# Attention and routed experts on one core: keys and queries turned by 64x64 products instead of transposes

## The chip, the cores and the metric

The kernel runs on one core of a Trainium2 chip. The core has engines that work side by side: TensorE (PE in the profile; PEld are its weight loads), VectorE (DVE), ScalarE (ACT), GpSimd (POOL) and SyncE (SP), which here only issues transfers. Products leave TensorE through PSUM, a memory of eight banks of 512 floats on each of 128 partitions; the operands lie in SBUF. The metric is the device time of one execution in microseconds (us). Three runs of the kernel before gave 433.92, 434.18 and 436.34 us; the median, 434.18, is its time here. One more execution was profiled.

## The reference

Two stages. The first is attention for 8 batches and 8 heads, 576 tokens, head width 64, causal by blocks of 64 tokens:

```python
scores = scale * np.matmul(q, k.transpose(0, 1, 3, 2))
mask = block_i >= block_j                      # blocks of 64 tokens
attn = softmax(where(mask, scores, -1e9))
out  = attn @ v
```

The second takes the 512 values of each token (its 8 heads side by side) and routes the token to one of 8 experts. `logits = x @ w_gate` choose a fresh expert; a local gate, a sigmoid of `x @ w_local`, decides per token whether it takes the fresh one or that of the token before it, so choices run on along the sequence. The chosen expert is two products with a ReLU between them:

```python
h = np.maximum(x[b, s] @ w1[e], 0.0)
out[b, s] = p[e] * (h @ w2[e])                 # p: softmax of the logits
```

All inputs and the output are float32.

## The kernel before

**Pairs and slots.** Two heads of one batch make a pair; there are 32 pairs and the main loop has one slot for each (`for i in range(NPAIR)`), four slots to a batch. The two heads lie on partitions 0 to 63 and 64 to 127 of a tile, so the products of both run in different parts of the 128x128 array. A slot i does, in TensorE's order: the values product of pair i-1 (`values`, L937), scores of pair i in three units (`scores`, L901 and L903; L901 is a small product that puts a large negative number where the mask is), the scores of the last 64 tokens (`last_scores`, L923), the transposes of keys and queries of pair i+1 (`transposes`, L860 and L856), and then a task of the batch before. ACT takes the exponentials of the scores out of PSUM (L913, L926), and copies the finished values (L941) and the turned keys and queries (L851). DVE adds the exponentials of the chunks into one tile (L949), for the row sums.

**Keys and queries.** Scores need both with the head's 64 numbers on the partitions, but they arrive with tokens on the partitions. `load_qk` issues the loads on SP: 512 tokens as [128 partitions, 2 heads, 4 tokens, 64], partition p holding tokens 4p to 4p+3, and the last 64 tokens ("the tail") of keys and queries in a small tile `qkl`. The large ones land in `staged`, a part of the second expert weights' tile `w2_bf` that isn't loaded yet. Two copies on POOL (`arrange`, L822) put the four tokens outermost, so that both heads of one token index make a 128x128 block. TensorE turns eight such blocks (L856) into a PSUM pair `kq` and the tail (L860) into the tile `po`. DVE copies the tail out (L862), ACT the rest (L851); that copy (`back_in_order`) reads in a row and writes every fourth float, because token 4s+j stands in block j. `qkTs[i % 2]` holds the result.

**PSUM.** The eight banks are three pairs under the name `sc` that go round, and `po` with two banks: the tail in its first columns, the last scores, the values. A wait is made between engines that touch the same bank of one tile. In a slot without more work the pairs go to the three score units and `kq`; a task takes the next ones. `bank_of` hands out banks: it takes a new pair when none is half used, or always for a step of the routing (names that begin with `rt`), and gives its two halves in turn. `half.clear()` forgets a half that is left.

**Tasks and routing steps.** `tasks(i)` gives by the quarter r of the batch: r = 0 and 2 a gate product (`half_batch`, L703), r = 1 the logits (L725) and rows of tiles 0 and 1, r = 3 the rows of tiles 2 and 3 and then of tile 4 (`rows_out`, L717), each with its transposes. Batch 0 has none but that of r = 2. The routing itself (`early`, `tokens`, `slots_first`) is a generator whose DVE pieces are put into the slots by weight; a piece that begins with work of TensorE waits for a call of `steps.tensor()`, of which a slot has two, one ahead of the task and one behind it. Such steps are L330, L340, L350, L363, L497.

**Weights.** `load_weights` brings one layer of one expert, 1 MB as bfloat16, over POOL's queue, in every second slot from slot 2 on. On that queue it stands behind `arrange`.

**Before and behind the loop.** Ahead of the loop, pair 0 is loaded, arranged by DVE and ACT (L1045), turned, and copied in four parts (L1061). Slot 1 has another order (`swap`): its scores come ahead of the values of pair 0. After the loop the tiles of 128 routed tokens pass through the experts (L1011, L1169); this part is the same in both kernels.

Of the kernel before, what the change touches and what calls it, by code (L numbers as in the profile page):

```python
# [62 lines left out]
def kernel(  # L63
# [11 lines left out]
    nc = tc.nc  # L75
# [29 lines left out]
    def load_weights(e, layer):  # L105
        if layer == 0:
            nc.gpsimd.dma_start(
                out=w1_bf[:, e * WE:(e + 1) * WE].rearrange("p (do f) -> p do f", f=F),
                in_=moe_w1[e].rearrange("(do di) f -> di do f", di=P))
        else:  # L110
            nc.gpsimd.dma_start(
                out=w2_bf[:, e * WE:(e + 1) * WE].rearrange("p (fo d) -> p fo d", d=Dm),
                in_=moe_w2[e].rearrange("(fo fi) d -> fi fo d", fi=P))

# [658 lines left out]
    with tc.tile_pool(name="atn_const", bufs=1) as cst, \  # L773
# [15 lines left out]
        def staged_of(i):  # L789
            return second if i == 1 else staged  # L790
# [8 lines left out]
        def load_qk(i):  # L799
# [16 lines left out]

        def arrange(i, copies):
            if i >= NPAIR:
                return
# [30 lines left out]
        def back_in_order(i, parts, ps, copy):  # L850
            copy(qkTs[i % 2][:, parts, :512].rearrange("p a (s j) -> p a j s", j=4),  # L851
                 ps.rearrange("p a (j s) -> p a j s", j=4))

        def turn_part(i, part, ps, js=range(4)):
            for j in js:
                nc.tensor.transpose(ps[:, j * P:j * P + P],  # L856
                                    raws[i][1 + part][:, j].rearrange("s h d -> s (h d)"), id_f)

        def turn_tail(i):
            nc.tensor.transpose(po[:, TAIL:TAIL + P],  # L860
                                raws[i][0].rearrange("s h d -> s (h d)"), id_f)
            nc.vector.tensor_copy(qkTs[i % 2][:, :, 512:S],  # L862
                                  po[:, TAIL:TAIL + P].rearrange("p (a s) -> p a s", a=2))

        def transposes(i, copy, ahead=0):
# [5 lines left out]
            for j in range(9):  # L871
                if j == ahead:
                    turn_tail(i)
                if j < 8:
                    turn_part(i, j // 4, ps[:, j // 4], (j % 4,))
            back_in_order(i, slice(0, 2), ps, copy)
# [474 lines left out]
```

## Time and profile before

| what | value |
|---|---|
| median of three runs | 434.18 us |
| time of the profiled execution | 430.82 us |
| its span, first to last instruction | 429.0 us |
| TensorE clock granted, mean | 0.999 |
| busy: PE, PEld | 412.7, 292.6 us |
| busy: DVE, ACT, POOL | 255.6, 264.2, 162.5 us |
| the 30 ACT copies of turned keys and queries (L851) | 63.1 us |
| the 61 POOL copies that arrange them (L822) | 40.0 us |
| the 256 transposes of keys and queries (L856) | 34.0 us busy |

How to read it: a row of the groups has line, engine, operation, out<-in by the program's names, the shape, the number of instructions, then the time the group was busy, the mean of one in ns, and the idle time of its engine ahead of it with what ended that. `128*128` or `64*64` is the part of the array that a product uses. PE's times of one matmul hold its latency, so neighbours overlap, and a float32 product shows as two matmuls. The chain of waits follows back from the last instruction to what released it; the timeline merges neighbours of a kind and gives start, duration and, in brackets, idle time. `w_bf` stands for both weight tiles, `staged` among them.

### The profile page before, as it was taken

What the parts mean: (1) busy time and instruction counts of PE and PEld (TensorE: products, weight loads), DVE (VectorE), ACT (ScalarE), POOL (GpSimd) and SP (SyncE); (2) the same over time, 40 slices, a digit from 0 to 9 for tenths busy, and PEclk for the clock granted to TensorE, in tenths of its full rate; (3) what the DMA queues carried; (4) which work ended last, traced back from release to release, by engine and by line L of the source; (5) the groups of instructions that cost most, each with busy time, mean ns of one, the idle gap of its engine ahead of it and who ended that gap; (6) DMA issues with size and microseconds to landing.
All of it is one profiled execution on the core that took longest, in us unless ns stands there. A gap on an engine that the chain in (4) does not pass through costs nothing.

```text
span 429.0 us, 13472 instructions
## 1 busy us (share of the span) xinstructions
PE 412.7 (96%) x5285; PEld 292.6 (68%) x5306; DVE 255.6 (60%) x558; ACT 264.2 (62%) x409; POOL 162.5 (38%) x181
## 2 busy tenths in 40 slices
PE   8999999999999999999999999899989999999995
PEld 7666767667667666676665767667767777777763
DVE  3363654565366386867899977698798433333320
ACT  4779668757776776566675667634445555555553
POOL 1216111221311121103113143016685788888843
PEclk9999999999999999999999999999999999999999
DMA  6578979989979999698998899957474555575541
GB/s 187 125 169 183 174 171 212 177 196 174 191 169 202 186 193 181 130 149 187 205 162 202 173 181 226 148 117 139 125 160 130 135 159 138 148 147 153 126 113 74
DMA packets 114366, 69.90 MB, mean 163 GB/s; under 512 B 77567, under 2 KB 106751, under 8 KB 114304
## 3 DMA queue, kind: packets, MB, share of 16 engines
q1 hardware_dynamic: 96896, 38.07, 39.3%
q0 software_dynamic: 17408, 30.96, 36.9%
q8 instruction: 44, 0.72, 0.7%
q14 instruction: 18, 0.15, 0.1%
HBM read 66.88 MB, written 14.70 MB: 190 GB/s over the span
## 4 chain that ended last, share of the span: by engine, by line
PE 76%; DVE 9%; DMA 6%; ACT 4%; issue 3%; POOL 1%; POOLq 0%; SPq 0%; DVEq 0%; ACTq 0%
PE o L937 19%; PE sc L903 16%; PE ps_h L1011 12%; PE ps_y L1169 11%; PE trg L703 5%; DMA out_dram<-y,idx 5%; PE kq L856 4%; PE trx L717 4%; ACT Pc L913 3%; DVE S L949 3%; PE o L860 2%; DMA xT<-xg 1%; PE sc L901 1%; PE trl L725 1%; PE idle L1032 1%
## 5 line engine op out<-in xcount | busy, mean ns | idle before, releaser
L822 POOL COPY w_bf<-w_bf 128x512 f32<-128x512 f32 x61 | 40.0, 668 | 197.1 <-PE kq L856 86.4
L949 DVE TENSOR_TENSOR S<-S,Pc 128x896 f32<-128x896 f32 (+3 forms) x128 | 90.2, 705 | 14.3 <-PE o L937 8.9
L903 PE MATMUL sc<-qkT 64*64 64x224 f32 (+6 forms) x1536 | 90.6, 366 | 0.0
L1220 DVE COPY w1c<-w_bf 128x4096 bf16 x36 | 44.9, 1246 | 55.9 <-PE ps_h L1011 52.8
L1011 PEld LDWEIGHTS <-w1c 128*128 128x128 bf16 x1152 | 67.2, 98 | 10.2 <-DVE w1c L1220 1.5
L1169 PE MATMUL ps_y<-w_bf,hT 128*128 x283 | 67.6, 379 | 1.1
L1011 PE MATMUL ps_h<-xT,w1c 128*128 128x128 bf16 x1088 | 66.3, 219 | 2.1 <-DMA xT<-xg 1.1
L1177 POOL DMA_INDIRECT out_dram<-y,idx x38 | 58.7, 1545 | 22.6 <-issue 9.8
L903 PEld LDWEIGHTS sc<-qkT 64*64 64x64 f32 x1536 | 59.8, 133 | 7.8
L913 ACT ACTIVATE Pc<-sc 128x448 f32<-128x448 f32 (+1 forms) x96 | 63.8, 703 | 0.0
L851 ACT COPY qkT<-kq 128x1024 f32<-128x1024 f32 x30 | 63.1, 2103 | 0.7 <-PE kq L856 0.7
L941 ACT COPY oT<-o 128x576 f32<-128x576 f32 x32 | 20.5, 639 | 69.2 <-PE o L937 66.4
L1014 ACT ACTIVATE hT<-ps_h 128x512 bf16<-128x512 f32 x76 | 45.3, 597 | 23.9 <-PE ps_h L1011 23.2
L653 POOL DMA_INDIRECT xg<-x_rows,idx x38 | 45.5, 1198 | 37.2 <-DVE ltmp_g L378 16.1
L937 PE MATMUL o<-Pc,v 128*64 128x320 f32 (+2 forms) x512 | 57.3, 366 | 0.0
L1174 ACT ACTIVATE y<-ps_y,xg 128x512 f32<-128x512 f32 x38 | 26.2, 689 | 43.7 <-PE ps_y L1169 38.5
L913 ACT ACTIVATE S<-sc 128x576 f32<-128x576 f32 x64 | 41.7, 652 | 15.3 <-PE o L923 11.8
L937 PEld LDWEIGHTS o<-Pc,v 128*64 128x64 f32 x512 | 34.6, 137 | 24.1
L1169 PEld LDWEIGHTS <-hT 128*128 128x128 bf16 x304 | 28.2, 98 | 27.7 <-issue 0.5
L937 PE MATMUL o<-S,v 128*64 128x256 f32 (+1 forms) x256 | 38.1, 418 | 0.9 <-DVE qkT L862 0.9
L856 PE MATMUL kq<-id_f,w_bf 128*128 128x128 f32 x256 | 34.0, 276 | 0.0
L862 DVE COPY qkT<-o 128x128 f32<-128x128 f32 x32 | 9.3, 290 | 37.9 <-PE o L860 37.7
(288 smaller groups left out, 416.0 us busy)
## 6 DMA issues: line engine op xcount, KB each, us to landing
w_bf<-in_moe_w_dram POOLq DMA_DIRECT2D x16, 1024.0 KB, 10.5
w_bf<-in_k_dram SPq DMA_DIRECT2D x32, 256.0 KB, 3.5
w_bf<-in_q_dram SPq DMA_DIRECT2D x32, 256.0 KB, 5.0
v<-in_v_dram SPq DMA_DIRECT2D x64, 128.0 KB, 4.2
x_rows<-xg SPq DMA_DIRECT2D x24, 128.0 KB, 3.6
qkl<-in_k_dram SPq DMA_DIRECT2D x32, 32.0 KB, 5.4
qkl<-in_q_dram SPq DMA_DIRECT2D x32, 32.0 KB, 4.1
vl<-in_v_dram SPq DMA_DIRECT2D x32, 32.0 KB, 3.6
```

The costliest lines, as they stand in the source:

```text
L653: st = nc.gpsimd.indirect_dma_start(out=x, out_offset=None, in_=x_dram[:rows], in_offset=bass.IndirectOffsetOnAxis(ap=row_of(ph, j), axis= ...
L851: copy(qkTs[i % 2][:, parts, :512].rearrange("p a (s j) -> p a j s", j=4), ps.rearrange("p a (j s) -> p a j s", j=4))
L856: nc.tensor.transpose(ps[:, j * P:j * P + P], raws[i][1 + part][:, j].rearrange("s h d -> s (h d)"), id_f)
L903: nc.tensor.matmul(to[:, col + skip:col + n], lhsT=t[r, 0, k0:k0 + ST], rhs=t[r, 1, q0 + skip:q0 + n], start=True, stop=True)
L913: nc.scalar.activation(exps_at(i, c, q0, n, rows), ps[rows, :, col:col + n], func=AF.Exp, scale=scale_attn)
L937: nc.tensor.matmul(po[64 * h:64 * h + 64, VO + q0:VO + q0 + n], lhsT=vv, rhs=exps_at(i, c, q0, n, slice(0, P))[:, h, :], start=(c == 0), s ...
L949: nc.vector.tensor_add(Ss[i][rows, :, P * c:], Ss[i][rows, :, P * c:], Pc[i % 2][rows, :, POS[c]:POS[c] + n])
L1011: nc.tensor.matmul(ps[:, fo, :], lhsT=w[:, ko * F + f0:ko * F + f0 + P], rhs=xT[:, ko, :], start=(ko == 0), stop=(ko == KO1 - 1))
L1014: relu[0] = nc.scalar.activation(hT[:, half * (FO // 2):(half + 1) * (FO // 2), :], ps, func=AF.Relu)
L1169: nc.tensor.matmul(ps, lhsT=hT[:, fo, :], rhs=w2_bf[:, bass.ds(ev + fo * Dm, Dm)], start=(fo == 0), stop=(fo == FO - 1))
L1177: st = nc.gpsimd.indirect_dma_start(out=out_flat, out_offset=bass.IndirectOffsetOnAxis(ap=row_of(ph, j), axis=0), in_=y, in_offset=None, b ...
L1220: ended["w"] = nc.vector.tensor_copy(w, w1_bf[:, bass.ds(ev[i], WE)])
```

## The change

1. `arrange` is gone, ahead of the loop too, and with it POOL's copies and the second staging place; `staged` now has four places for raw keys and queries, those of even and of odd pairs.
2. The transposes of 128x128 blocks become products with a 64x64 identity (`flip`). `turn_part` makes four for each part and token index: two halves of the partitions (r) by two heads (h). Each reads the raw block as it was loaded, uses one 64x64 quarter of the array, and writes 64 columns, every fourth float, of bank r. So the tokens come out in order.
3. The tail is turned by four such products into the first and the last columns of `po`, one in each of its banks, and copied by ACT in place of DVE.
4. The large copy reads and writes runs of 256 floats.
5. `bank_of` no longer takes a new pair for a routing step; the halves are forgotten only ahead of the two calls of `steps.tensor()`. So a step and the task behind it share a pair. In quarter 3 tile 4 comes first.
6. `load_weights` gets a wait for the slot's large copy (`kept[0]`).

```diff
-    def load_weights(e, layer):
+    def load_weights(e, layer, behind=None):
...
+        if behind is not None:
+            tc.add_manual_dep(st.ins, behind.ins.name, mybir.DependencyInfo(
+                mybir.DependencyClass.Sync, mybir.DependencyReason.DATA),
+                reason="spread over the slots")
...
-        staged, second = (w2_bf[:, e * WE:(e + 1) * WE].bitcast(F32).rearrange(
-            "p (u c) -> p u c", u=4) for e in (E - 1, E - 2))
+        staged = w2_bf[:, (E - 1) * WE:E * WE].bitcast(F32).rearrange("p (u c) -> p u c", u=4)
...
-                m = staged_of(i)[:, j].rearrange("p (h j d) -> p h j d", h=2, j=4)
+                m = staged[:, 2 * (i % 2) + j].rearrange("p (h j d) -> p h j d", h=2, j=4)
...
-        def arrange(i, copies):
-            for j in range(2):
-                m = staged_of(i)[:, 2 + j].rearrange("p (j h d) -> p j h d", j=4, h=2)
-                copies[j](m, raws[i][1 + j].rearrange("p h j d -> p j h d"))
-                raws[i][1 + j] = m
...
-            if not half or nm.startswith("rt"):
-                half.clear()
+            if not half:
...
-        def back_in_order(i, parts, ps, copy):
-            copy(qkTs[i % 2][:, parts, :512].rearrange("p a (s j) -> p a j s", j=4),
-                 ps.rearrange("p a (j s) -> p a j s", j=4))
+        def flip(out, src, rows):
+            nc.tensor.matmul(out, lhsT=src, rhs=id_f[rows, rows], start=True, stop=True)
+
+        quarters = [(r, h, slice(64 * r, 64 * r + 64), slice(64 * h, 64 * h + 64))
+                    for r in range(2) for h in range(2)]
 
         def turn_part(i, part, ps, js=range(4)):
             for j in js:
-                nc.tensor.transpose(ps[:, j * P:j * P + P],
-                                    raws[i][1 + part][:, j].rearrange("s h d -> s (h d)"), id_f)
+                for r, h, rows, to in quarters:
+                    flip(ps[to, r].rearrange("p (a s j) -> p a j s", a=2, j=4)[:, part, j],
+                         raws[i][1 + part][rows, h, j], rows)
 
         def turn_tail(i):
-            nc.tensor.transpose(po[:, TAIL:TAIL + P],
-                                raws[i][0].rearrange("s h d -> s (h d)"), id_f)
-            nc.vector.tensor_copy(qkTs[i % 2][:, :, 512:S],
-                                  po[:, TAIL:TAIL + P].rearrange("p (a s) -> p a s", a=2))
+            tail = po.rearrange("p (a s) -> p a s", s=P)[:, 0::7, :ST]
+            for r, h, rows, to in quarters:
+                flip(tail[to, r], raws[i][0][rows, h], rows)
+            nc.scalar.copy(qkTs[i % 2][:, :, 512:S], tail)
...
-            back_in_order(i, slice(0, 2), ps, copy)
+            kept[0] = copy(qkTs[i % 2][:, :, :512].rearrange("p a (r s) -> p r a s", r=2),
+                           ps.rearrange("p r (a s) -> p r a s", a=2))
...
             if r == 3 and b:
-                return [[lambda t=t: rows_out(b - 1, t) for t in (2, 3)],
-                        [lambda: rows_out(b - 1, 4)]]
+                return [[lambda: rows_out(b - 1, 4)],
+                        [lambda t=t: rows_out(b - 1, t) for t in (2, 3)]]
...
-            turn_part(0, part, ps[:, 0])
-            for s0, s1 in ((0, FIRST[part]), (FIRST[part], P)):
-                copies[part](
-                    qkTs[0][:, part, 4 * s0:4 * s1].rearrange("p (s j) -> p j s", j=4),
-                    ps[:, 0].rearrange("p (j s) -> p j s", j=4)[:, :, s0:s1])
+            turn_part(0, part, ps)
+            for r in range(2):
+                copies[part](qkTs[0][:, part, QA * r:QA * r + QA],
+                             ps[:, r, QA * part:QA * part + QA])
         turn_tail(0)
         idle_products(2)
-        arrange(1, (nc.vector.tensor_copy, nc.gpsimd.tensor_copy))
...
+            half.clear()
             steps.tensor()
             steps.vector(2.0)
             for group in tasks(i):
-                half.clear()
...
+            half.clear()
             steps.tensor()
...
-            arrange(i + 2, [nc.gpsimd.tensor_copy] * 2)
...
-                load_weights(*divmod(wload, 2))
+                load_weights(*divmod(wload, 2), behind=kept[0])
```

More of the change, by code (lines that the diff above doesn't have):

```diff
@@ L1039 @@
         copies = (nc.vector.tensor_copy, nc.scalar.copy)
-        for part in range(2):
-            raw, m = raws[0][1 + part], staged[:, 2 + part].rearrange(
-                "p (j h d) -> p j h d", j=4, h=2)
-            for n, j in enumerate((slice(0, 2), slice(2, 4))):
-                copies[part * (1 - n)](m[:, j], raw[:, :, j].rearrange("p h j d -> p j h d"))
-            raws[0][1 + part] = m
         load_qk(1)
```

12 lines of the change are left out of this document (4 added, 8 removed).

## The prediction

> **What bounds the kernel now.** I read the page first (busy times and the chain that ended last), then the chain of waits in order of time for two slots of the attention stage, then the timeline of one slot, the groups by shape and the list of waits. TensorE (PE) is busy nearly always and carries the chain:
>
> ```profile
> span 429.0 us, 13472 instructions
> PE 412.7 (96%) x5285; PEld 292.6 (68%) x5306; DVE 255.6 (60%) x558; ACT 264.2 (62%) x409; POOL 162.5 (38%) x181
> PE 76%; DVE 9%; DMA 6%; ACT 4%; issue 3%; POOL 1%; POOLq 0%; SPq 0%; DVEq 0%; ACTq 0%
> ```
>
> The change lies in the attention stage, where PE walks through 32 slots of about 8.5 us. The chain in one slot (start, duration, what):
>
> ```profile
> 115.72 0.26 PE o L860
> 115.98 0.87 PE kq L856 x8
> 116.85 0.67 PE trl L725 x6
> 117.52 0.04 issue
> 117.56 1.09 PE trx L717 x8
> 118.65 2.85 PE o L937 x28
> ```
>
> Behind the scores come the tail transpose (L860) and the eight key and query transposes (L856), then the task of the slot and the values product (L937); only 0.04 us is not PE. So what decides is how long PE takes from its last score to its last key or query transpose, 0.26 + 0.87 = 1.13 us, and who waits next. The timeline of the slot before it (start, duration, engine, line):
>
> ```profile
> 105.15 0.33 PE L923 MATMUL o<-qkT 64*64 64x64 f32 x4
> 105.27 1.08 PE L903 MATMUL sc<-qkT 64*64 64x288 f32 x16
> ...
> 106.60 0.33 ACT L926 ACTIVATE Pc<-o 64x64 f32<-64x64 f32 x2
> 107.15 0.33 PE L860 MATMUL o<-id_f,qkl 128*128 128x128 f32 x1
> 107.32 1.04 PE L856 MATMUL kq<-id_f,w_bf 128*128 128x128 f32 x8
> 107.50 1.45 ACT L913 ACTIVATE Pc<-sc 128x448 f32<-128x448 f32 x2
> 108.28 0.16 PEld L703 LDWEIGHTS trg<-oT,wg 128*32 128x32 f32 x8 [0.17 <-issue]
> 108.83 2.16 ACT L851 COPY qkT<-kq 128x1024 f32<-128x1024 f32 x1
> 110.03 1.19 PE L937 MATMUL o<-S,v 128*64 128x256 f32 x8
> ```
>
> **Products in place of transposes.** A transpose is one instruction. A float32 product shows as two passes: L923 has two products in a slot and four matmul rows. So 8 + 1 transposes become 32 + 4 products, 72 passes with 72 weight loads: 18 passes on each of the four 64x64 tiles. From the first L923 row to the next line is 0.12 us, in which each of two tiles makes two passes of 64 columns: 0.06 us a pass, loads included. The streaming alone comes from the slope of two shapes, and whether four tiles run side by side from a third answer, for 9.20 to 9.30 us:
>
> ```profile
> L903 PE MATMUL sc<-qkT 64*64 64x288 f32 x384 | 44.8, 415 | 0.0
> L903 PE MATMUL sc<-qkT 64*64 64x128 f32 x128 | 13.3, 284 | 0.0
> ...
> 9.27 0.47 PE L903 MATMUL sc<-qkT 64*64 64x288 f32 x4
> L903 PE MATMUL sc<-qkT 64*64 64x288 f32 x4 | 0.5, 453 | 0.0
> ```
>
> (415 - 284) / 160 = 0.82 ns a column, 52 ns for 64. Four products of 453 ns fit into 0.47 us, so all four tiles start within 0.02 us. I take 56 ns, between 52 and 60: 18 x 0.056 = 1.01 us in place of 1.13, a gain of 0.12 (0.05 to 0.19). Part of it is that the new products have the tile shape of the scores before them.
>
> Does the sequencer bring 144 instructions in 1.01 us, 7 ns each? The eight L703 loads take 0.16 us, of which one lasts 0.11: 0.05 us for seven steps, 7 ns. The other end is the 0.12 us behind L923's first row, four passes and four loads, 15 ns each; but there the streaming of two tiles sets the pace. I take the first and keep the other for the rivals.
>
> The new products write every fourth float of a PSUM bank; no row shows such a write. Below, it is free; above, the nearest row is the copy that writes SBUF at the same step:
>
> ```profile
> L851 ACT COPY qkT<-kq 128x1024 f32<-128x1024 f32 x30 | 63.1, 2103 | 0.7 <-PE kq L856 0.7
> L913 ACT ACTIVATE Pc<-sc 128x1024 f32<-128x1024 f32 x32 | 33.0, 1031 | 0.0
> L913 ACT ACTIVATE Pc<-sc 128x448 f32<-128x448 f32 x64 | 34.5, 538 | 0.0
> L862 DVE COPY qkT<-o 128x128 f32<-128x128 f32 x32 | 9.3, 290 | 37.9 <-PE o L860 37.7
> ```
>
> 2103 against 1031 ns for as many elements, a factor of 2.04: a pass of 0.11 us, 16 x 0.056 = 0.90 us more a slot. I take the free end: bf16 products stream two columns, 8 bytes a partition, in the time in which a float32 pass streams one. The row for it:
>
> ```profile
> 289.05 1.07 PE L1011 MATMUL ps_h<-S,w1c 128*128 128x128 bf16 x16
> ```
>
> About 1.07/16 = 0.067 us for 128 columns with the last one's latency in it, 0.52 ns a column against 0.82. So a bank takes 8 bytes a partition in 1.04 ns there, and a stepped pass would ask it for one float in 0.82 ns: nearly the same number of places in the same time. The Trainium skill (PSUM — Partial Sum Buffer, Specifications (TRN2)) says that PSUM has cachelines of 8 bytes and that "any non-contiguous AP slows matmuls significantly". By that rule the sum would be that of the first rival below; by the bf16 row a stepped pass touches one line where bf16 touches one too, and stays at 0.056. No run here shows a stepped product.
>
> How much of 0.12 us reaches the end depends on the slot. In slots with a gate task (quarter 0 and 2 of a batch, 15 of them) only PE is on the chain: 15 x 0.12 = 1.8 us. In quarter 1 the row task waits for the exponentials (the 0.04 us above), so nothing is gained; quarter 3 fills two banks and then needs the same buffer: nothing.
>
> **The copies.** ACT's 2.10 us copy becomes contiguous, 1.03 us. The tail copy leaves DVE (0.29) for ACT: by the two L913 rows 0.86 ns an element over 155 ns, 0.27 us for 128. ACT's queue: exponentials to 108.95, tail 109.22, keys and queries 110.25 rather than 110.99. The next scores come when the values product is through, 110.03 + 2.85 = 112.9, so this hides, as does POOL's copying (61 x 0.67 us), which no PE row waits for. What is new: the values product writes the banks that the tail copy reads and now waits for ACT, behind the exponentials. With a task that is covered (109.22 against 110.03). Slot 3 has none:
>
> ```profile
> 33.11 1.04 PE L856 MATMUL kq<-id_f,w_bf 128*128 128x128 f32 x8
> 33.34 1.46 ACT L913 ACTIVATE Pc<-sc 128x448 f32<-128x448 f32 x2
> 34.07 1.19 PE L937 MATMUL o<-S,v 128*64 128x256 f32 x8
> ```
>
> Exponentials end at 34.80, the copy at 35.07, and 0.04 us later the product: 1.0 us lost, once (0 if the dependence isn't made). The tail, now in two banks, must wait for both L926, which end at 106.93; PE comes to it at 107.15 today, 0.12 earlier at most then. Nothing.
>
> **Routing steps.** PE's idle time in the stage (total, times, longest):
>
> ```profile
> PE trx L717 <- ACT Pc L913: 2.3, 4, 0.8
> PE trg L703 <- ACT Pc L913: 2.0, 4, 0.6
> PE o L937 <- DVE qkT L862: 0.9, 2, 0.8
> PE rtr L363 <- ACT qkT L851: 0.8, 2, 0.4
> ```
>
> Three bank pairs go round. Today a routing step takes the second score pair and the task behind it the third, whose exponentials end last. Sharing the pair, the gate task starts at once: 2.0 us. For the row tasks only the short tile 4, put first, fits beside the step: four transposes at 0.87/8 = 0.11, 0.43 us of each wait, 1.7 in all. The wait for L862 was DVE being late with the tail copy, 0.8 gone. L363 waits for the key and query copy, which ends 0.74 earlier: 0.5 of 0.8. Sum 5.0 us (from 2, if the next wait takes over, to 6). With the pair shared, both halves must be read before the fourth next user; DVE reads within 2 us and the next use is a slot away: nothing.
>
> **The start.** Pair 1 is turned in slot 0, copied by DVE, and slot 1 begins:
>
> ```profile
> 8.63 0.34 ACT Pc L926 x2
> 9.01 0.34 PE o L860
> 9.67 1.97 DVE qkT L851
> 11.69 0.22 PE sc L901 x2
> ```
>
> The DVE copy ends at 11.64 and lets slot 1 start. It loses the tail copy ahead of it (0.29) and, at L913's ratio, half of its 1.97: up to 1.3 us, and PE could start about 10.4. But the exponentials of slot 0 and the rest of its scores also stand between, which no quoted row bounds; I put half, 0.65 us (0 to 1.3).
>
> **Transfers.** The key and query loads keep their place on SP's queue, ahead of the value loads and row stores, but wait for the products of two pairs earlier, done a slot before, instead of POOL's copy.
>
> ```profile
> w_bf<-in_k_dram SPq DMA_DIRECT2D x32, 256.0 KB, 3.5
> w_bf<-in_q_dram SPq DMA_DIRECT2D x32, 256.0 KB, 5.0
> ```
>
> Landing takes 3.5 and 5.0 us, and they have over one slot: nothing. The weight load waits for ACT's copy (110.25); POOL issues it at about that point today behind its copies, and what queues behind it on POOL, the next weights and the first gathers, is a slot or more away: nothing.
>
> **Sum**, on the profiled execution's own 430.82 us (span 429.0): -1.8 - 5.0 + 1.0 - 0.65 = -6.45, 424.4. The median of the runs is 434.18, 3.36 above that execution; the same step from it gives 427.7 us.
>
> **The rivals.**
> 1. *The stepped PSUM write doubles a pass* (slower). The products then take 1.91 us, 0.78 more than today's 1.13, in 30 slots: +23.4; the other terms give back 5.0 + 0.65 - 1.0 = 4.65: 434.2 + 18.7 = 452.9. Its place is the product that follows L856; it decides from the point where those 16 passes eat 4.65/30 + 0.12 = 0.275 us, a pass of 56 + 17 = 73 ns. For it: no row shows the write free, and SBUF's stepped copy costs 2.04. Against it: the bf16 rate. Chance 0.20.
> 2. *The sequencer is the limit.* At 15 ns an instruction the 144 take 2.16 us, 1.03 more than today: +30.9 - 4.65, 460.4; at 10 ns 1.44, +9.3 - 4.65, 438.8. The loads at 7 ns speak against it. Chance 0.10. The Trainium skill (TensorE: Matmul & The Clock Gate, "Wait — 56ns, not 53.3ns?") states that matmuls never start less than about 25 ns apart; held over all tiles, that would make 72 x 25 = 1.8 us, 0.67 more than today, and by the same working 449.6. The four products that start within 0.02 us disagree with it for a burst; no row shows it over 1 us.
> 3. *The gains are covered.* The exponentials (to 108.95 in a slot whose transposes end at 108.3) hold back the tasks as the third pair does now, and PE's gain turns into waits: of the sum stay the start, slot 3 and a third of the routing gain, -0.65 + 1.0 - 1.7 = -1.35: 432.8. For it: quarter 1 already waits. Against: gate slots show 110.03 against 108.95. Chance 0.14.
>
> **How the numbers follow.** My forecast has 0.56, and its own range, from the ends of its terms, is 424 (-2.9 - 6 + 0 - 1.3) to 432 (-0.8 - 2 + 1.0). A measurement of this kernel tells about 0.5%, 2.2 us, from no change. Faster: the forecast and a little of the third, 0.57; within 0.5%: the rest of the third, 0.13; slower: the first and second, 0.30. As that is more than 2 in 10, the range reaches over the first rival: 423 to 455.
>
> **What would show it.** A pass of the new 64-column products at about 56 ns and 1.0 us from last score to last product; no L822; the ACT copy near 1.03 us; slot 3's L937 idle by 1 us behind ACT; the L703 and L717 waits gone or shorter; slot 1's scores about 1 us earlier. A pass above 73 ns, or PE idle behind issue in the products, would make me wrong, and so would a wait of L937 for the tail copy in every slot.

## The result and the profile after

The changed kernel takes 448.81 us (median of four runs, 447.29 to 449.76) against 435.26 of before on the same chip: a ratio of 1.0308, 95% interval 1.0253 to 1.0362. It is 3% slower. The forecast was 427.7 us and faster; the time lies in the range given (423 to 455) and the direction is wrong. The profiled execution took 449.73 us.

The page of the changed kernel, its span, busy times, instruction transfers and the chain by engine:

```profile
span 447.9 us, 17384 instructions
PE 419.0 (94%) x7301; PEld 302.7 (68%) x7322; DVE 240.3 (54%) x522; ACT 234.5 (52%) x440; POOL 112.9 (25%) x120
q8 instruction: 60, 0.98, 0.9%
PE 59%; issue 15%; POOL 11%; DVE 6%; DMA 6%; POOLq 1%; SPq 1%; ACT 1%; DVEq 0%; ACTq 0%
```

The same queue in the kernel before (packets, MB, share):

```profile
q8 instruction: 44, 0.72, 0.7%
```

Two things stand out. "Issue", time in which an engine waits for nothing that the profile shows, has gone from 3% of the chain to 15%. Most of that lies in the experts' stage, where the chain that ended last now runs over POOL's transfers; up to the first expert product (298 us) issue is 3.9% of the chain, against 2.6% in before (up to 282 us). And the engines' own instructions now come in 60 transfers where they came in 44. 0.98 MB in 60 is 16 KB each. The groups of the new lines by shape (count, busy us, mean ns, idle time ahead):

```profile
L843 PE MATMUL kq<-id_f,w_bf 64*64 64x64 f32 x2048 | 38.7, 222 | 3.9 <-issue 3.8
L871 ACT COPY qkT<-kq 128x1024 f32<-128x1024 f32 x30 | 31.6, 1052 | 2.3 <-PE kq L843 1.9 <-ACT qkT L858 0.3
L858 ACT COPY qkT<-o 128x128 f32<-128x128 f32 x32 | 9.1, 285 | 1.3 <-PE o L843 1.3
```

The copies are what the prediction said, 1.05 us in place of 2.10 and 0.29 for the tail. The products have idle time behind issue ahead of them. The chain of waits of two slots, the first with such a hole and the second without (start, duration, what):

```profile
106.82 0.16 PE o L843 x6
106.97 0.59 PE kq L843 x40
107.57 1.43 issue
108.99 0.58 PE kq L843 x24
109.57 0.57 PE trx L721 x4
110.14 0.02 issue
110.17 0.69 DVE xg L768
110.86 0.04 issue
110.90 1.09 PE trx L721 x8
...
117.61 0.16 PE o L843 x6
117.77 0.94 PE kq L843 x64
118.71 1.75 PE trg L707 x24
```

The slot at 117 is the one that was forecast: tail and flips 1.10 us where the transposes took 1.13. A stepped pass takes 0.94/16 = 59 ns on each of the four tiles. The slot at 107 shows both ways in which time was lost. In the middle of the flips PE stands still for 1.43 us. Then the row task turns four blocks, waits for DVE to read them (0.69 us), and only then turns the other eight.

Where the time went by place: the last values product of the attention stage starts at 278.52 us before and at 294.86 after, 16.3 later. The experts' stage adds 2.6, but two profiles of one and the same kernel below differ there by 6.0, so nothing is read from that.

**A stop that nothing in the program asks for.** I numbered PE's profiled instructions (products and weight loads) and took every gap of over 0.38 us between two starts that no wait accounts for. In the attention stage of the changed kernel these gaps lie at instruction 1451, 3223, 3981, 4235, 7523, 7776, 9293 and 10051: each is 184 to 187 beyond a multiple of 253, so they come at fixed places of an even division of PE's instructions, some 253 profiled ones to a part. The 14,623 of them make 58 such parts, about as many as there are 16 KB transfers. With the sequencer's own 531 instructions counted too, each of the eight lies 193 beyond a multiple of 256, and so do the stops of the other kernels. I take these places for the bounds of instruction packets of 256. And each gap ends 2.2 to 2.5 us after the start of an instruction transfer (3.5 in one case, whose transfer took 2.0 us itself and not about 1.0). Such a stop I call a stall at a bound. The sum for all kernels of this study, up to 300 us (each gap less 0.1 us; the delay is the median time from PE's start on one packet to the start of the transfer that brings the next):

```
kernel             instructions  stalls  sum us  delay us
before                  10.6k       0      0       1.7
step_turn               10.6k       0      0       1.3
step_again              10.6k       0      0       1.8
pairs_alone             10.6k       0      0       1.5
dense                   14.6k       3      2.4     1.7
spread                  14.6k       1      0.8     1.6
earlier                 14.6k       4      2.7     1.8
flips_best              14.6k       6      7.7     1.8
sep_tail                14.6k       6      7.9     2.0
shifted                 14.7k       5      8.3     1.9
after                   14.6k       8     10.8     2.6
sep_pairs               14.6k      10     11.0     2.0
halves                  14.6k      11     14.2     2.2
no_weight_loads         14.6k       0      0       0.9
flips_no_loads          14.6k       0      0       0.9
before_no_loads         10.6k       0      0       0.0
```

The row of `halves` is from a slow execution (452.5 us, where its fast ones take 445.3 to 446.9) and is not compared with the others. A stall comes where PE is through a packet before the next one's delay and the 2.2 us or more behind it are over. In before a packet lasts PE 7.9 us at least and 9.3 in the median, while the delays reach 3.8, so all of it stays hidden. In after a packet lasts 3.6 us at least and 6.4 in the median, and the delays reach 5.4.

The Trainium skill (Runtime: NRT & Kernel Launch, Instruction fetch mechanics) says that an engine's instructions are refilled in 16 KiB blocks of 256, over a DMA queue, while the current block runs, and that the cost at a block's end is "mostly hidden". The 256 agree with the trace. That the cost is hidden held here for the kernel of 10.6 thousand instructions and not for the changed one's 14.6 thousand: 10.8 us.

### The profile page after: what moved, and what is told of

It reads as the page before. It is cut to its first block, busy times and chain, and to the rows that moved or that the text cites. A ratio compares the mean times of both kernels' runs of the same rounds, so it can differ in the third digit from the quotient of the medians.

```text
span 447.9 us, 17384 instructions
## 1 busy us (share of the span) xinstructions
PE 419.0 (94%) x7301; PEld 302.7 (68%) x7322; DVE 240.3 (54%) x522; ACT 234.5 (52%) x440; POOL 112.9 (25%) x120
## 4 chain that ended last, share of the span: by engine, by line
PE 59%; issue 15%; POOL 11%; DVE 6%; DMA 6%; POOLq 1%; SPq 1%; ACT 1%; DVEq 0%; ACTq 0%
PE o L935 19%; PE sc L901 16%; POOL out_dram L1164 7%; PE kq L843 6%; DMA out_dram<-y,idx 5%; PE trg L707 5%; POOL xg L657 4%; PE trx L721 3%; DVE S L947 2%; PE ps_h L1009 2%; PE trl L729 1%; PE rta L707 1%; PE sc L899 1%; PE ps_y L1156 1%; DMA qkl<-in_k_dram 1%
## 5 line engine op out<-in xcount | busy, mean ns | idle before, releaser
L947 DVE TENSOR_TENSOR S<-S,Pc 128x896 f32<-128x896 f32 (+3 forms) x128 | 88.4, 691 | 26.9 <-PE o L935 21.3
L901 PEld LDWEIGHTS sc<-qkT 64*64 64x64 f32 x1536 | 61.2, 133 | 6.8
L657 POOL DMA_INDIRECT xg<-x_rows,idx x38 | 49.0, 1291 | 47.9 <-DVE S L947 14.6
L935 PE MATMUL o<-Pc,v 128*64 128x320 f32 (+2 forms) x512 | 58.6, 371 | 0.8 <-issue 0.8
L935 PEld LDWEIGHTS o<-Pc,v 128*64 128x64 f32 x512 | 35.7, 139 | 25.5 <-issue 2.7
L1164 POOL DMA_INDIRECT out_dram<-y,idx x38 | 45.3, 1192 | 23.7 <-issue 9.7
L843 PE MATMUL kq<-id_f,w_bf 64*64 64x64 f32 x2048 | 38.7, 222 | 3.9 <-issue 3.8
L111 POOL DMA_DIRECT2D w_bf<-in_moe_w_dram x8 | 7.2, 900 | 130.0 <-ACT qkT L871 119.6
L107 POOL DMA_DIRECT2D w_bf<-in_moe_w_dram x8 | 6.3, 790 | 129.1 <-ACT qkT L871 93.7
L843 PEld LDWEIGHTS kq<-id_f,w_bf 64*64 64x64 f32 x2048 | 34.9, 137 | 5.0 <-issue 5.0
```

What stands on the lines that cost most here:

```text
L657: st = nc.gpsimd.indirect_dma_start(out=x, out_offset=None, in_=x_dram[:rows], in_offset=bass.IndirectOffsetOnAxis(ap=row_of(ph, j), axis= ...
L843: nc.tensor.matmul(out, lhsT=src, rhs=id_f[rows, rows], start=True, stop=True)
L901: nc.tensor.matmul(to[:, col + skip:col + n], lhsT=t[r, 0, k0:k0 + ST], rhs=t[r, 1, q0 + skip:q0 + n], start=True, stop=True)
L935: nc.tensor.matmul(po[64 * h:64 * h + 64, VO + q0:VO + q0 + n], lhsT=vv, rhs=exps_at(i, c, q0, n, slice(0, P))[:, h, :], start=(c == 0), s ...
L947: nc.vector.tensor_add(Ss[i][rows, :, P * c:], Ss[i][rows, :, P * c:], Pc[i % 2][rows, :, POS[c]:POS[c] + n])
L1164: st = nc.gpsimd.indirect_dma_start(out=out_flat, out_offset=bass.IndirectOffsetOnAxis(ap=row_of(ph, j), axis=0), in_=y, in_offset=None, b ...
```

## The experiments

All ratios are against the kernel before on the same chip; its median went from 430.5 to 435.6 us between chips, so ratios are compared, not times.

### The shared bank pair

First the changed kernel with part of the change undone:

```diff
-            if not half:
+            if not half or nm.startswith("rt"):
+                half.clear()
...
-                return [[lambda: rows_out(b - 1, 4)],
-                        [lambda t=t: rows_out(b - 1, t) for t in (2, 3)]]
+                return [[lambda t=t: rows_out(b - 1, t) for t in (2, 3)],
+                        [lambda: rows_out(b - 1, 4)]]
...
-            half.clear()
             steps.tensor()
             steps.vector(2.0)
             for group in tasks(i):
+                half.clear()
```

> The changed kernel with the routing steps given a bank pair of their own again and the row tasks in their old order; products, copies and weight loads as changed. Theory A (PE runs out of fetched instructions in the dense flips, and that is most of the loss): the four waits of L721 for DVE at about 1.0 us go, 446 to 443 us, and idle time of PE behind issue stays near 12 us in the attention stage, though in other slots. Rival P (sharing the pair is the loss): back to 434 to 436 us, near the kernel before.

Measured: 443.57 us, ratio 1.0253 (1.0207 to 1.0299). The last values product starts at 289.60, 5.3 us earlier than after, and L721's waits for DVE are gone. The stalls kept their sum, 11.0 us. A holds, P falls: the shared pair is a part of the loss and not most of it.

Then the same part alone, put into the kernel before (the diff above the other way round, on before):

> The kernel before with the shared bank pair and the new order of the row tasks alone; transposes, arranging and loads as before. Theory W (sharing takes PE's waits for the exponentials away and puts waits for DVE in their place): L703's and L717's waits for ACT go, L717 waits for DVE by 1.0 us in four row tasks, and the sum is a loss of 0 to 4 us against before. Rival (the prediction's term): 5.0 us faster, 429 against 434.

Measured: 439.47 us, ratio 1.0193 (1.0134 to 1.0252), so 8 us slower; of these 5.3 lie in the attention stage (last values product at 283.81 against 278.52). The rest is in the experts' stage and is not read, as above. Theory W named the right thing and put its price too low; the prediction's -5.0 is out. The list of PE's waits in this kernel (total, times, longest), its five longest in the attention stage:

```profile
PE rta L703 <- DVE w_bf L332: 2.5, 2, 1.5
PE trx L717 <- DVE xg L764: 2.3, 3, 0.8
PE rtr L363 <- ACT qkT L850: 1.4, 2, 0.7
PE rtd L717 <- DVE lt_g L352: 0.9, 1, 0.9
PE rti L717 <- DVE w_bf L499: 0.8, 1, 0.8
```

The 2.3 and 2.0 us of L717 and L703 behind the exponentials are gone, as forecast. But more waits for DVE have come. The chain of one row slot shows why, first in this kernel, then in before:

```profile
65.96 0.87 PE kq L855 x8
66.84 0.45 PE trx L717 x4
67.29 0.02 issue
67.31 0.69 DVE xg L764
68.01 0.04 issue
68.05 0.98 PE trx L717 x7
```

```profile
65.61 0.87 PE kq L856 x8
66.49 1.34 PE trx L717 x12
67.82 1.22 PE o L937 x9
```

Before, twelve transposes in a row. With the shared pair tile 4 goes to one half, tile 2 to the other half of the same pair and tile 3 to a new pair. Tile 2, and tile 3 behind it, wait until DVE has read tile 4. The two halves are different banks, and still PE waits: the wait is made over the whole tile of two banks. My description of the kernel, by which a wait is made between engines that touch the same bank of a tile, is wrong in this. It costs 0.97 us in each of the three quarter-3 slots (8.08 to 9.05 us) and in the last, and as much in a slot where a routing step takes the first half (9.43 to 10.40).

### The number of instructions

The changed kernel with its later instructions moved by about half a packet:

```diff
-        idle_products(7)
+        idle_products(5)
+        few = psp.tile([P, 2, 512], F32, tag="sc", name="few")
+        for j in range(32):
+            nc.tensor.matmul(few[:64, 0, :1], lhsT=zeros[:64, :64], rhs=zeros[:64, :1],
+                             start=True, stop=True)
```

> The changed kernel with 32 tiny products (64 instructions of loads and 64 of passes) ahead of slot 0 in place of two idle products, so that every later instruction of PE lies half a packet of 256 further on. Theory A: the stalls behind issue of 1.4 to 2.1 us move to other slots (not 80, 107, 189, 235 us), their sum stays between 6 and 16 us, and the time is 442 to 454 us. Rival (the stalls belong to the work of those slots, a task, a weight load or a transfer): they stay in the same slots with the same sizes, and the time is within 1 us of the changed kernel.

Measured: 457.58 us, ratio 1.0622 (1.0563 to 1.0682), 3.6 us beyond A's range; 6.7 us of it lie ahead of the first values product (21.11 against 14.39), where the tiny products run; from there to the last values product it takes 1.2 us less than after. The stalls stand at 74, 139, 204, 250 and 290 us, none in a slot that had one before, and by instruction number all at 184 to 188 beyond a multiple of 253. So a stall belongs to a place in the row of instructions and not to the work of a slot. One of them in the chain, near the end of the flips:

```profile
73.02 0.94 PE kq L843 x62
73.96 2.02 issue
75.98 0.32 PE kq L843 x2
```

The kernel before with as many instructions more, and nothing else:

```diff
+            for j in range(8):
+                for r in range(2):
+                    for h in range(2):
+                        rows, to = (slice(64 * x, 64 * x + 64) for x in (r, h))
+                        nc.tensor.matmul(ps[to, r, j:j + 1], lhsT=id_f[rows, rows],
+                                         rhs=id_f[rows, :1], start=True, stop=True)
             for j in range(9):
```

> The kernel before with 32 products of one column added ahead of the eight transposes of each slot, 64 passes and 64 weight loads, results overwritten by the transposes; nothing else differs. Theory A: the number of instructions alone does it. 128 instructions at 7 ns are 0.9 us a slot, 28 us in 31 slots, and on top of that come stalls behind issue at packets' bounds of 6 to 12 us in all: 465 to 475 us. Rival (the stalls belong to something else in the change, its waits or its copies): 456 to 462 us and no idle time of PE at bounds.

Measured: 460.06 us, ratio 1.0557 (1.0487 to 1.0627). In the attention stage it is 24.4 us longer, 0.79 a slot, which is 6.1 ns for each of the 128 instructions, stalls included. There are three stalls, 2.4 us. So instructions alone make stalls where before has none, but far fewer than A said and than after has; the time lies in the rival's range, the stalls that the rival excluded are there.

Then the flips taken apart, with separate pairs and the tail on DVE (`sep_tail` below is the same without it): tail and keys behind the scores, queries behind the slot's task:

```diff
-                transposes(i + 1, nc.scalar.copy, 6 if swap else 0)
+                transposes(i + 1, nc.scalar.copy if swap else None, 6 if swap else 0)
...
+            queries()          # turn_part(i, 1, ps) and the copy
             slot[0] = i + 0.5
```

> The kernel with separate pairs and the tail on DVE, and the flips taken apart: tail and keys behind the scores, the queries behind the slot's task, one copy of both after that. The instructions of a slot are the same, but no more than about 72 of the flips come in one go. Theory A (a stall comes where PE goes through instructions faster than packets arrive): stalls at the packets' bounds in the attention stage fall from 8 to 11 us to under 3, and two more changes of tile shape a slot cost up to 0.15 us each: 434 to 440 us. Rival (what counts is the number of instructions in a slot, not how close they come): the stalls keep their sum, 444 to 450 us.

Measured: 452.03 us, ratio 1.0363 (1.0307 to 1.0419). The stalls fell to 0.8 us, as A said, and the time didn't. PE's waits in this kernel:

```profile
PE trg L707 <- ACT Pc L926: 5.2, 14, 0.6
PE trx L721 <- ACT Pc L926: 3.4, 7, 0.8
PE trl L729 <- ACT Pc L926: 1.7, 6, 0.3
```

With only the keys ahead of it, each task comes half a microsecond earlier and meets the exponentials that hold the third pair: 10.3 us of waits, where before has 4.3 (the rows of L703 and L717 in the prediction). The rest had stood hidden behind the turning of the queries. So part of the gain was given back in another wait: 6.0 of the 17.3 us by which the attention stage is longer than before's. The chain of waits also has the half of the flips that stands alone behind a task, at 0.62 us where half of 0.94 is 0.47. What makes up the remainder was not followed up, and the time missed both ranges.

### Slot 3

The kernel with separate pairs, and the tail's copy on DVE:

```diff
-            nc.scalar.copy(qkTs[i % 2][:, :, 512:S], tail)
+            nc.vector.tensor_copy(qkTs[i % 2][:, :, 512:S], tail)
```

> As the one with separate pairs, and the tail's copy back on DVE. Theory A2 (in slot 3 the values product waits for ACT behind the exponentials, and the clock that halves for 3.4 us behind that wait doubles its price): 2 to 3 us less than with separate pairs alone, slot 3 back from 10.2 to about 8.6 us and no half-clock stretch. Rival: the gap of 2.38 us in slot 3 is a late instruction packet, and the time stays within 1 us of the kernel with separate pairs.

Measured: 445.67 us, ratio 1.0365 (1.0281 to 1.045), against 1.0253 for `sep_pairs`: no gain. (The profiled execution is the fastest of the four; its last values product comes 3.4 us ahead of that of `sep_pairs`, 3.1 of it from fewer stalls.) The gap ahead of slot 3's values product is still there, and it is behind issue:

```profile
32.80 0.81 PE L844 MATMUL kq<-id_f,w_bf 64*64 64x64 f32 x43
35.68 1.19 PE L936 MATMUL o<-S,v 128*64 128x256 f32 x8 [2.06 <-issue]
```

In after the same gap looks like a wait for ACT:

```profile
32.97 1.12 PE L843 MATMUL kq<-id_f,w_bf 64*64 64x64 f32 x64
34.65 0.29 ACT L858 COPY qkT<-o 128x128 f32<-128x128 f32 x1
34.79 1.06 ACT L871 COPY qkT<-kq 128x1024 f32<-128x1024 f32 x1
36.25 1.36 PE L935 MATMUL o<-S,v 128*64 128x256 f32 x6 [2.17 <-ACT qkT L871]
```

but the copies end at 34.94 and 35.85, and the product starts 0.4 us after the later one. It lies at instruction 1451, a packet's bound. The rival is right on the gap, though not on the time (2.1 us apart, where it said 1): the gap is a late packet, and the wait for the tail is inside it. In `shifted`, where no bound falls there, that wait can be seen by itself:

```profile
41.37 0.29 ACT L858 COPY qkT<-o 128x128 f32<-128x128 f32 x1
41.70 1.19 PE L935 MATMUL o<-S,v 128*64 128x256 f32 x8 [0.90 <-ACT qkT L858]
```

The slot is 0.93 us longer than before's (7.68 against 6.75): the 1.0 us of the prediction. In after the gap also has a second price. Its stretches from the gap on (start and end, PE busy, PEld, DVE, ACT, POOL, granted clock, share of transfers, GB/s):

```profile
33.80:36.60 2.80, 0.63 (x24) 0.42 (x18) 0.00 (x0) 2.05 (x4) 0.00 (x0) 1.00 1.11 202
36.60:40.00 3.40, 3.40 (x20) 1.77 (x18) 1.64 (x2) 0.00 (x0) 0.00 (x0) 0.50 0.89 238
40.00:55.00 15.00, 15.00 (x344) 11.02 (x340) 5.88 (x17) 10.26 (x20) 0.96 (x1) 1.00 0.73 133
```

For 3.4 us behind it the clock was 0.50, so the values product took 1.7 us more. In `sep_tail` the gap is 2.28 us and the clock stays at 1.00; in `sep_pairs` it is 1.46 and the clock stays too, so theory A2's half-clock stretch wasn't there to be saved.

### What makes a packet late

If a transfer's way into PE has its own length, it should not matter what else is on the queues. The changed kernel without its weight loads:

```diff
-                load_weights(*divmod(wload, 2), behind=kept[0])
+                e, layer = divmod(wload, 2)
+                nc.gpsimd.memset((w2_bf if layer else w1_bf)[:, e * WE:(e + 1) * WE], 0.0)
```

> The changed kernel with the fourteen 1 MB weight loads of the attention stage left out; POOL sets the weights to zero instead, so the expert products' values are not the reference's. Theory A (a packet's way into PE has its own length): stalls at the packets' bounds stay, 8 to 12 us in the attention stage, each still ending 2.2 to 2.6 us after the start of a packet. Rival (packets are late because they queue behind the weight transfers): under 4 us of stalls remain and the first expert product comes at 287 us or earlier, not 298.

Measured: 446.70 us, with no stall at a bound in the attention stage: theory A's "fixed length" falls, if it is counted from PE's start on the packet before. Counted from the transfer's own start it isn't tested: in no kernel did PE come to a packet less than 2.2 us after that. The time says little (the first expert product comes at 292.8 us and not by 287), since POOL sets its zeros in one go from 37 us on and DVE, which then stands still too, holds PE up for 6.7 us at 48 us. Two kernels with shorter or earlier bursts of the same bytes followed:

```diff
-                load_weights(*divmod(wload, 2), behind=kept[0])
+                load_weights(*divmod(wload // 2, 2), behind=kept[0], part=wload % 2)   # half, each slot
```

> The changed kernel with each 1 MB weight load cut into two of 512 KB, one a slot, tied in the same way: the same bytes, in bursts of half the length. Without the weight loads the median packet started 1.0 us after PE had come to the bound before it, with them 2.7. Theory Q (a packet waits in the queues behind the transfers that were issued ahead of it, so the length of a burst counts): stalls at bounds in the attention stage fall from 10.7 to under 6 us, the time by 4 us or more, to 445 or less. Rival (only the share of time in which transfers run counts): stalls 8 to 12 us, the time within 2 us of the changed kernel.

Measured: 446.91 us, ratio 1.0275 (1.0225 to 1.0326), within after's interval. The profile of this kernel can't be compared, so its stalls decide nothing. By the time, theory Q, that the length of a burst counts, has nothing for it: it forecast 4 us or more.

```diff
-            kept[0] = copy(qkTs[i % 2][:, :, :512]...
+            copy(qkTs[i % 2][:, :, :512]...
...
+                if u == 0:
+                    kept[0] = st           # the slot's first exponentials
```

> The changed kernel with each weight load tied to the slot's first exponentials in place of the key and query copy: it starts 3 to 4 us earlier, ahead of the flips and not behind them. Theory T (the tie behind the copy sets the loads where the packets of the next flips are fetched): stalls at bounds fall under 5 us. Rival (the place in the slot does not matter, as a load lasts 7 to 10 us, more than a slot): 8 to 12 us again, at other bounds, and the time stays between 445 and 452 us.

Measured: 443.51 us, ratio 1.0215 (1.0165 to 1.0266), stalls 2.7 us. That looked like T. So the flips were given the best of everything, separate pairs, the tail on DVE and this tie:

> The changed kernel with separate pairs, the tail's copy on DVE, and the weight loads tied to the first exponentials: only the flips, the contiguous copy and the end of POOL's arranging are left of the change. Theory (loads tied there leave under 4 us of stalls at bounds): last values product at 278 to 282 us, the time within 1% of before. Rival (the low sum of stalls with that tie was the phase of one program): stalls of 8 to 12 us again and a ratio near 1.025.

Measured: 447.26 us, ratio 1.035 (1.0274 to 1.0427), stalls 7.7 us. The rival holds: the low sum of `earlier` was the phase of one program. This kernel also shows another late transfer, in a slot that takes 13.4 us where before has 9.57:

```profile
PE kq L844 <- issue: 3.4, 3, 1.2
PE o L844 <- DMA qkl<-in_k_dram: 3.1, 1, 3.1
```

The tail of the keys, issued at 204.4 us, landed 9.6 us later. The waits of PE for this load are 0.7 us in after, 1.2 in `sep_pairs`, 1.8 in `sep_tail` (the queries' tail) and none in before.

Last the pair of kernels without weight loads, on before and on the flips with separate pairs and the tail on DVE:

> The kernel before with the fourteen weight loads of the attention stage left out and the weights set to zero by POOL, so that the expert products' values are not the reference's. It is the base for the next kernel; since before has no stalls at bounds, its slots should keep their 8.55, 8.08 and 9.4 us where POOL's setting of zeros (some 14 us a quarter of them) does not hold up its arranging.

> The changed kernel with separate pairs and the tail's copy on DVE, likewise without the weight loads. Theory D (packets are late behind the weight transfers): no stall at a bound after 70 us, gate slots 8.46 us and row slots 8.17 to 8.47, and from the ninth values product to the last 2 to 4 us less than the same stretch of before (202.2 us). Rival (the run without loads was lucky in its phase): stalls of 3 us or more in that stretch, and a stretch as long as before's or longer.

Measured: 435.19 us in the profiled execution of the first and 445.24 of the second; both have long waits for DVE while POOL sets zeros, 12.2 us in the second, so their whole times compare nothing. Behind these the second has no stall at all, as theory D said. PE's waits in it, longest first, have no row behind issue:

```profile
PE o L936 <- DVE qkT L859: 12.2, 2, 12.0
PE ps_h L1010 <- ACT LT L715: 2.8, 1, 2.8
PE trx L721 <- ACT Pc L912: 2.3, 4, 0.8
```

From the ninth values product to the last it takes 200.15 us where before (with loads) takes 202.22: 2.07 less, at the lower end of D. The first kernel is no base for this stretch, as waits of PE for DVE lengthened three of its slots by 0.7 to 2.6 us. Of the 2.07, 1.08 are the two slots in which L363 waits for the copy (9.66 to 9.12 and 9.57 to 9.03), and 0.92 is the one slot in which before's values product waits for DVE's tail copy (L862; 9.39 to 8.47). The products themselves give next to nothing: a gate slot without routing goes from 8.55 to 8.46 us, a quarter-3 slot from 8.08 to 8.17, and most slots of the routing stay as they are.

So the weight transfers make the packets later. Two programs of 14.6 thousand instructions without them have no stall and a median delay of 0.9 us each, eight with them and as many instructions have 0.8 to 11.0 us of stalls and a delay of 1.6 to 2.6. The kernel before shows the same, 0.0 us without them and 1.7 with them, but its packets last long enough to hide it. How the delay comes about is not settled. Some stalls of after (at 80 and 189 us) lie where no weight load is under way, between one's end and the next one's start, so it is not simply the load in front in the queue.

### The step in PSUM alone

The kernel before, whose transposes write every fourth float:

```diff
-            copy(qkTs[i % 2][:, parts, :512].rearrange("p a (s j) -> p a j s", j=4),
-                 ps.rearrange("p a (j s) -> p a j s", j=4))
+            copy(qkTs[i % 2][:, parts, :512], ps)
...
-                nc.tensor.transpose(ps[:, j * P:j * P + P],
+                nc.tensor.transpose(ps.rearrange("p (s j) -> p j s", j=4)[:, j],
```

> The kernel before with one edit: its eight transposes write every fourth float of the bank, so that ACT's copy reads and writes without a step; arranging, pairs and loads as before. Theory S (a stepped PSUM write of a 128x128 transpose is free, as the 64-column passes are): L856's group keeps about 1.04 us a slot, the copy goes from 2.10 to 1.03 us, and the time falls by 0.5 to 2 us, 432 to 434.5. Rival (a transpose with a stepped write takes double): 0.87 us more in 30 slots, about 460 us. Second rival: nothing waits for the copy, within 0.3 us of before.

Measured: 429.43 us, ratio 0.9973 (0.9938 to 1.0009). Its groups:

```profile
L855 PE MATMUL kq<-id_f,w_bf 128*128 128x128 f32 x256 | 34.3, 277 | 0.1
L851 ACT COPY qkT<-kq 128x1024 f32<-128x1024 f32 x30 | 31.0, 1032 | 0.7 <-PE kq L855 0.7
```

A stepped transpose has a mean of 277 ns, a plain one 276. Theory S holds, and the gain is where it should be: 0.66 us ahead of the first values product and 0.54 in each of the two slots in which L363 waits for the copy.

> The kernel before with transposes that write every fourth float, run a second time over more rounds. If the slots 0 (0.66 us), 18 and 22 (0.54 us each) are what it gains, the ratio is 0.994 to 0.997; if the first figure was chance, 1.000.

Measured over more rounds: 433.62 us, ratio 0.9943 (0.9914 to 0.9972). It is faster than both kernels, against before by about half a per cent, and it is the one part of the change that was seen to pay.

## Why the prediction was wrong, step by step

- **What bounds the kernel.** Right: TensorE's chain decides in nearly every slot, and each loss shows in it.
- **Products in place of transposes, -1.8 us.** The price of a pass was right (56 ns taken, 59 measured), and so was 7 ns an instruction: 64 passes with their loads in 0.94 us. The term was too large all the same. Six gate slots gave 0.09 us instead of 0.12, those of the routing 0.04 or nothing, and three quarter-3 slots, put at nothing, lost 0.09: about 0.3 us where nothing stalls.
- **The rate of the sequencer.** This is the step that failed first. I asked whether PE can take 144 instructions in a microsecond and not whether they are there. The trace of before had the answer's half: the instruction queue's 44 packets. The row stood on the page, and I didn't ask what 4,000 more instructions make of it. It cost 10.8 us, and it was in no term and in no rival; only the list of signs had it ("PE idle behind issue in the products"). Rival 2 priced the instructions' rate, where the 7 ns held, and would have had every slot slower and not eight.
- **The stepped PSUM write, taken as free.** Right, for 64-column products and for 128-column transposes. The Trainium skill's rule on non-contiguous patterns (PSUM — Partial Sum Buffer, Specifications (TRN2)) is not borne out by the 277 against 276 ns, and rival 1, which it would have borne out, falls.
- **The floor of 25 ns between matmuls** of the Trainium skill (TensorE: Matmul & The Clock Gate, "Wait — 56ns, not 53.3ns?"). The runs disagree if it is held over all tiles: 64 passes in 0.94 us are 14.7 ns apart.
- **The copies, nothing.** Right for ACT and POOL: the ACT copy takes 1.05 us.
- **Slot 3, +1.0 us.** Right as a term, 0.93 where it stands alone. In after it lies inside a stall and half a clock, 3.9 us over slot 3 and the one behind it.
- **Routing steps, -5.0 us.** The 3.7 us of it that hung on the shared pair had the wrong sign: +5.3. The step that failed is "DVE reads within 2 us and the next use is a slot away: nothing". The next use is not of the pair but of its other half, in the same task, and it waits for DVE's read. I had bounded the term below by 2 us of gain; with the wait made over the whole tile it had no such bound. The other two terms held: the wait for L862 is gone (0.8 forecast, 0.92 in its slot), and so is that of L363 (below).
- **The start, -0.65 us.** 0.66 in `step_turn`, where nothing else is changed; that it comes so near is luck, as I had put half of a range, and part of the range was DVE's tail copy, which `step_turn` keeps. In after the first values product starts at 14.39 against 14.45: nothing is left of it, for a reason that I did not follow up.
- **L363, -0.5 us.** Right in kind and put at half of what came: twice 0.54, as the copy ends earlier.
- **Transfers, nothing.** Wrong by 0.7 us: once in the routing slots PE waits for the tail of the keys.
- **Rival 3, the gains are covered.** Not what happened in after, but `spread` shows the mechanism: as soon as PE gets to a task earlier, the exponentials hold it.

The account of the attention stage, against +16.3: stalls 10.8 (slot 3's wait for the tail among them), half a clock 1.7, the shared pair 5.3, a late load 0.7, together 18.5; L363 -1.1, L862 -0.9 and the flips -0.3 leave 16.2. That the sum comes out so even is partly luck, as several terms are taken from other kernels than after and overlap in single slots.

## What to carry to other kernels

Count a change's instructions as well as its cycles: a dense run of small products can outrun the supply of instructions, and the page shows it as idle time behind "issue" ahead of these products and as more packets of the instruction queue, while whether a given slot stalls depends on where the packets' bounds fall, so one program's luck is not a result. When two users share a tile, look at what a wait is made over, the tile or the part, before a gain is written down for the sharing. And where work hides a wait, as the flips hid the exponentials, moving the work shows the wait.

## What was not expected of the hardware

- PE's instructions come 256 at a time in transfers of 16 KB, and where PE stood waiting for one it went on 2.2 to 2.5 us after that transfer's start in nearly every case, though the transfer itself takes about 1.0.
- With the fourteen 1 MB weight loads left out, these transfers start 0.9 us (median) after PE's start on the packet before, in both changed kernels without them; with them 1.6 to 2.6. In the kernel before it is 0.0 and 1.7.
- After a gap of 2.38 us the clock was 0.50 for 3.4 us; after one of 2.28 us in another kernel it stayed at 1.00. In `shifted` a stretch of 3.4 us at 0.50 began at 222.6 us, behind an idle time of 1.6 us, so the length of one gap alone does not decide it.
- Writing every fourth float of a PSUM bank costs a 128x128 transpose 1 ns of 276.
